# One more chunk's low weight parts by VectorE, and two ScalarE copies emitted later, in a gated mix of attention and GEGLU

## The chip, the cores and the metric

The kernel runs on one core of one Trainium2 chip. The metric is the device time of one execution in microseconds (us); less is better. Three runs of the kernel before took 595.72, 596.25 and 597.62 us, so the median is 596.25 us. The profile shows one further execution. In its lines PE is TensorE (PEld its weight loads), DVE is VectorE, ACT is ScalarE, POOL is GpSimd, and SP is the engine that only issues transfers. L689 is line 689 of the kernel before.

## The reference

For 2048 tokens of 512 channels the kernel computes a sliding, dilated attention (32 heads of 16 channels, 8 keys per token at a distance of 2), a GEGLU feed-forward network of 1792 hidden channels, and a gate that mixes them:

```python
g = _sigmoid((x * gate_w).sum(-1, keepdims=True))
a = _A_ref(x, A_wqkv, A_wo)          # attention and its output projection
b = (_gelu(x @ w_gate) * (x @ w_up)) @ w_down
return g * a + (1 - g) * b
```

All tensors are float32.

## The kernel before

**Tokens and parities.** The 2048 tokens are split into two halves by the parity of their position, since the keys of a token have its parity. Each half goes through the same stages: keys and queries, values (with the gate's logits), then the feed-forward network. `par` is 0 in the first parity and 1 in the second. The main function calls `values(0, ...)`, `ffn(0)`, `keys(...)` (for the second parity), `values(1, ...)` and `ffn(1)` in this order.

**Products.** Each block product is done with seven products of half the size instead of eight, from sums of quarters of both operands (names such as t1, t2, b11 for the weights, a11, s1 for the tokens). Each operand is kept as two numbers: a rounded high part, and a low part, raw minus high. A product takes three matmuls: high by high, high by low, low by high.

**Low parts, two ways.** `operands(par, f, i)` (L662 to L693) makes the weights of chunk f of the feed-forward network (14 chunks, f from 0) from the raw quarters in a tile `raw`. Group i = 0 has three quarters (768 columns), group i = 1 has four (1024 columns). In one way, ScalarE makes the high part (L678) and VectorE subtracts it from raw (L682). In the other, which this text calls "by transfer", ScalarE writes minus the high part into the place of the low part (L686), a GpSimd-issued transfer of 512 KB adds raw to it in memory (L689), and ScalarE makes the high part (L691). The function is a generator: the second half, after `yield`, is emitted at a later step. In the second parity, group 0 is loaded back from memory instead, where the first parity left it. Low parts of the hidden values (L749, L750 or L753) and of the down weights (L716, L718 or L720, L721) are made in the same two ways.

**Feed-forward.** `gate_up` (L794 to L845) works through one chunk: seven products on TensorE (`product`, L730), with evictions from PSUM by ScalarE (L735, L741, L812, L827, L843) and sums and products by VectorE (L742, L746). Between the products come pieces of other work: in chunks 0 and 1 the last two key products (`key_one`, matmuls at L460, evicted at L480 into a buffer `rt` and added into memory by two GpSimd-issued transfers, L465 and L466), and later `down` (L766, matmuls at L777), which multiplies hidden values by the down weights. The last group of `down` in the first parity scales its result by 1 - g while evicting it (L785) into a buffer that is then stored.

**Keys of the second parity.** `keys` (L416) follows the first parity's `down`. Its first product uses the four PSUM banks called `acc` (24 matmuls at L460), which are copied to four banks called `p` (L434, ScalarE); the second product (24 matmuls, `p<-d,A`) adds to these copies, and is evicted at L437. There are four `acc` and four `p` banks.

**Values.** `values` (L336 to L414) does seven products of four matmul groups each (matmuls at L348 with 258 columns; evictions by ScalarE at L355). After each of these 28 steps it calls `next(bg)`, so that a generator handed to it emits a little other work there. In the second parity this is `rest_b` (two steps), then empty steps, then `operands(1, 0, 1)`: the second group of chunk 0.

**Attention.** It runs on VectorE beside all this, as background work that is pulled in between (`pull`), with an exponential on ScalarE (L537).

**What sets the order.** The program is emitted in the order of the calls. A scheduler of the framework then decides, from costs of its own, in which order each engine gets its instructions; TensorE, VectorE and ScalarE run theirs strictly in that order, and so do the queues of the transfers. `paced` (L581) ties an instruction to the last matmul that was emitted before it, for the order only: the scheduler may not place it earlier than that. (In some stretches it also pins VectorE's instructions to their order of emission.) An instruction without it may be hoisted to any place where its operands and buffers allow.

Of the kernel before, what the change touches and what calls it, by code (L numbers as in the profile page):

```python
# [45 lines left out]
def tile_gated_mix(ctx: ExitStack, tc: tile.TileContext, xt, wqkv, wff, wo, out):  # L46
# [11 lines left out]
    def tl(tag, dt=F32):  # L58
        return pool.tile([P, COLS.get(tag, 512)], dt, name=tag, bufs=BUFS[tag])
# [151 lines left out]
    def room_b(name):  # L211
        if name in ("b11", "t2", "t4"):
            t = tl("g1", F32R)
            cols = [t[:, i * 512:(i + 1) * 512] for i in range(4)]
        else:
            cols = [*pair("d"), *pair("d")]
        for kc in range(2):
            QO[name, kc] = cols[2 * kc:2 * kc + 2]
# [7 lines left out]
    def split_b(name, kc):  # L226
        split(nc.vector, *QO[name, kc], QR[name, kc], held)
# [78 lines left out]
    def rest_b():  # L306
        room_b("b22")
        for kc in range(2):
            split_b("b22", kc)
            yield  # L310
# [270 lines left out]
    def paced(ins):  # L581

        if PIN[0] and ins.ins.engine == mybir.EngineType.DVE:
            tc.keep_in_program_order(ins)
        if not PACING[0]:
            return ins
        tc.add_manual_dep(ins.ins, LAST[-1].ins.name, mybir.DependencyInfo(mybir.DependencyClass.Sync,
                          mybir.DependencyReason.SCHED_ONLY), reason="pace")
        return ins
# [72 lines left out]
    def operands(par, f, i):  # L662


        n = len(GROUPS[i]) * QW
        w = tl(f"g{i}", F32R)
        hi, lo = w[:, :n], w[:, n:2 * n]
        for k, op in enumerate(GROUPS[i]):
            WG[f, op] = hi[:, k * QW:(k + 1) * QW], lo[:, k * QW:(k + 1) * QW]
        if par and not i:  # L670
            nc.sync.dma_start(w[:, :2 * n].bitcast(F32), WS[f, i])
            yield
            return
        raw = RAW[f][:, 3 * i * QW:][:, :n]
        if not i:
            KEEP[f] = w[:, :2 * n]
        if not i or (not par and f == 1):
            ins = nc.scalar.activation(hi, raw, AF.Copy)  # L678
            if f:
                paced(ins)  # L680
            yield
            ins = nc.vector.tensor_tensor(lo, raw, hi.bitcast(F32), op=OP.subtract)  # L682
            if f:
                paced(ins)
            return
        ins = nc.scalar.activation(lo, raw, AF.Copy, scale=-1.0)  # L686
        if par and not f:
            paced(ins)
        nc.gpsimd.dma_start(lo.bitcast(F32), raw, accum_op=OP.add)  # L689
        yield  # L690
        ins = nc.scalar.activation(hi, raw, AF.Copy)  # L691
        if par or f:
            paced(ins)  # L693
# [194 lines left out]
    def ffn(par):  # L888
        todo = iter(())
        for f in range(FC):  # L890
# [9 lines left out]
            if f + 1 < FC:  # L900
                for i in range(2):
                    steps = operands(par, f + 1, i)
                    at(1 + 2 * i, next, steps, None)
                    at(5 + i, next, steps, None)
                at(0 if f != 1 else 5, fetch_d, f + 1)
                for g_ in ((), (0, 1))[f] if f < 2 else (f,):
                    steps = down_w(par, g_)
                    at(2 if f > 2 else 4 - f % 2, next, steps, None)
                    at(7, next, steps, None)
            else:  # L910
                steps = down_w(par, f)
                at(1, next, steps, None)
                at(4, next, steps, None)
# [149 lines left out]
    for kc in range(KC):  # L1063
        name, i = ("b11", "b21")[kc // 2], kc % 2
# [134 lines left out]
    def first():  # L1199
        for _ in range(2):  # L1200
            yield
        combine(0)
        keep(0)
        for i in range(2):
            yield
            for _ in operands(0, 0, i):
                yield
        combine(1)
        fetch_d(0)
        yield  # L1210
        for n in "t1", "b22":
            room_b(n)
            for kc in range(2):
                if n == "t1":
                    combine_b("t1", "b11", "b22", "t2", kc)
                split_b(n, kc)
                yield
# [8 lines left out]
    def second():  # L1226

        yield from operands(1, 0, 0)
        room_v(*SMALL, *LARGE)
        for n in "b11", "b21", "t1", "b22", "t2":  # L1230
            fetch_v(n)
            yield
# [7 lines left out]
        if k < 2:  # L1240
            fetch_v(("t3", "t4")[k])

    values(1, chain(rest_b(), [None] * 9, operands(1, 0, 1)), again_v)
    ffn(1)


# [41 lines left out]
```

## Time and profile before

| what | value |
|---|---|
| three runs | 595.72, 596.25, 597.62 us |
| profiled execution | 596.87 us |
| its span, first to last instruction | 595.1 us |
| mean granted TensorE clock | 0.999 |
| VectorE busy | 533.3 us (90%) |
| L689 transfers (low parts by transfer) | 27, 512 KB each, median 6.1 us from issue to landing |
| L682 subtracts (low parts by VectorE) | 15, one of them 128x1024 |

The profiled execution's own time is 1.8 us longer than its span, and 0.62 us above the median of the three runs. A line of a timeline has the start, the duration, the engine, the line of the code, the operation, the output tile and its inputs, the shape, how many instructions run on without a break, and in brackets how long the engine was idle before it and what released it. On TensorE each matmul's duration overlaps the next one's; a new matmul of 512 columns starts every 0.227 us. On TensorE the first parity's feed-forward network runs from about 50 to 279 us, the second parity's keys (first five products) and values from 273 to 330 us, and its feed-forward network from 322 us on; they overlap somewhat at each change.

### The profile page before, as it was taken

To read this page: it belongs to the slowest core of one execution; us is meant where nothing else is said; L and a number is where in the kernel's file an instruction comes from. 1 tells how busy PE (TensorE), PEld (TensorE's weight loads), DVE (VectorE), ACT (ScalarE), POOL (GpSimd) and SP (SyncE) were. 2 spreads that over 40 slices of the span, in tenths; PEclk is the share of its full clock that TensorE was granted. 3 is DMA by queue.
4 is the path that set the end of the run, shared out by engine and by line. 5 is a ranking of instruction groups with operands and counts; after the bars stand their busy time and mean duration, and the time that the engine had idled before them with its cause. 6 is when DMAs were issued, how large, how long until landed. Compare 5 with 4: busy or idle time off the path is not lost.

```text
span 595.1 us, 8276 instructions
## 1 busy us (share of the span) xinstructions
PE 586.6 (99%) x2743; PEld 488.8 (82%) x2743; DVE 533.3 (90%) x622; ACT 429.4 (72%) x758; POOL 123.4 (21%) x144
## 2 busy tenths in 40 slices
PE   9999999999999999999999999999999999999997
PEld 7889887888888888887788888888888888888885
DVE  6989898999799996999996999799979988999891
ACT  6778786678887779777767665767696778796632
POOL 0130670112111112112001571112121212141200
PEclk9999999999999999999999999999999999999999
DMA  8689999989878988899889999889778988988725
GB/s 301 223 235 295 307 284 236 295 245 243 260 219 246 232 268 234 237 344 267 255 264 330 258 276 227 230 190 265 198 247 213 260 213 215 265 197 230 98 53 176
DMA packets 89464, 143.28 MB, mean 241 GB/s; under 512 B 8655, under 2 KB 49999, under 8 KB 89422
## 3 DMA queue, kind: packets, MB, share of 16 engines
q1 hardware_dynamic: 67470, 106.91, 54.6%
q0 software_dynamic: 21664, 35.46, 33.8%
q8 instruction: 21, 0.34, 0.3%
q10 hardware_dynamic: 288, 0.39, 0.2%
q14 instruction: 21, 0.17, 0.1%
HBM read 69.83 MB, written 46.49 MB: 195 GB/s over the span
## 4 chain that ended last, share of the span: by engine, by line
PE 90%; DMA 6%; DVE 1%; ACT 1%; issue 1%; SPq 0%; ACTq 0%; DVEq 0%
PE p L730 42%; PE p L777 13%; PE acc L777 12%; PE acc L460 10%; PE p L1002 5%; PE acc L348 3%; PE p L348 3%; DMA g<-raw 2%; PE acc L1002 2%; DMA v<-vs 1%; DMA raw<-ws 1%; PE p L460 1%; DMA vs<-hh 1%; DMA raw<-xt 1%; DVE raw L245 1%
## 5 line engine op out<-in xcount | busy, mean ns | idle before, releaser
L730 PE MATMUL p<-S,g 128*128 128x512 f32 x672 | 166.7, 389 | 0.0
L730 PEld LDWEIGHTS p<-S,g 128*128 128x128 f32 x672 | 126.0, 188 | 26.1
L730 PE MATMUL p<-A,g 128*128 128x512 f32 x504 | 125.1, 390 | 0.7 <-DMA g<-raw 0.7
L730 PEld LDWEIGHTS p<-A,g 128*128 128x128 f32 x504 | 94.3, 188 | 20.8 <-DMA g<-raw 1.1
L558 DVE TENSOR_TENSOR prod<-v,lg 128x2048 f32<-128x2048 f32 x32 | 72.9, 2279 | 0.8
L519 DVE TENSOR_TENSOR prod<-kq 128x2048 f32<-128x2048 f32 x32 | 72.9, 2278 | 0.6 <-DMA kq<-kq 0.3
L522 DVE TENSOR_REDUCE lg<-prod 128x128 f32<-128x2048 f32 x32 | 73.0, 2281 | 0.1
L777 PE MATMUL p<-d,hh 128*128 128x512 f32 x224 | 68.8, 389 | 0.0
L689 POOL DMA_DIRECT2D g<-raw x27 | 23.4, 867 | 188.9 <-ACT g L686 122.9
L741 ACT ACTIVATE c<-p 128x512 f32<-128x512 f32 x56 | 33.3, 597 | 38.9 <-PE p L730 38.6
L777 PE MATMUL acc<-d,hh 128*128 128x512 f32 x224 | 58.4, 390 | 0.0
L777 PEld LDWEIGHTS acc<-d,hh 128*128 128x128 f32 x224 | 42.0, 188 | 8.9 <-ACT hh L749 0.2
L777 PEld LDWEIGHTS p<-d,hh 128*128 128x128 f32 x224 | 42.1, 188 | 8.7
L742 DVE TENSOR_TENSOR c<-c,s 128x512 f32<-128x512 f32 x56 | 37.8, 683 | 5.6 <-ACT c L741 5.4
L777 PE MATMUL p<-d,hl 128*128 128x512 f32 x112 | 42.6, 389 | 0.0
L746 DVE TENSOR_TENSOR c<-c 128x512 f32<-128x512 f32 x56 | 38.3, 684 | 3.2 <-ACT c L843 3.1
L562 DVE TENSOR_TENSOR prod<-prod 128x1024 f32<-128x1024 f32 x32 | 39.1, 1221 | 0.3
L735 ACT ACTIVATE s<-p 128x512 f32<-128x512 f32 x56 | 33.0, 590 | 7.1 <-PE p L730 6.5
L721 POOL DMA_DIRECT2D d<-r x23 | 19.7, 858 | 86.6 <-ACT d L720 60.0
L460 PE MATMUL acc<-d,S 128*128 128x512 f32 x144 | 35.2, 390 | 0.6 <-ACT hh L1164 0.6
L790 ACT ACTIVATE rt<-p 128x512 f32<-128x512 f32 x48 | 28.1, 594 | 9.4 <-PE p L777 9.1
L777 PE MATMUL acc<-d,hl 128*128 128x512 f32 x112 | 34.5, 389 | 0.0
(220 smaller groups left out, 1065.0 us busy)
## 6 DMA issues: line engine op xcount, KB each, us to landing
g<-raw POOLq DMA_DIRECT2D x27, 512.0 KB, 6.1
ws<-g SPq DMA_DIRECT2D x14, 768.0 KB, 5.9
g<-ws SPq DMA_DIRECT2D x14, 768.0 KB, 7.0
r<-wff SPq DMA_DIRECT2D x28, 256.0 KB, 4.5
raw<-wff SPq DMA_DIRECT2D x14, 512.0 KB, 4.5
d<-r POOLq DMA_DIRECT2D x23, 256.0 KB, 6.5
ws<-raw SPq DMA_DIRECT2D x14, 384.0 KB, 4.9
raw<-ws SPq DMA_DIRECT2D x14, 384.0 KB, 4.9
```

The lines of the kernel that those rows point to most:

```text
L348: LAST[:] = [nc.tensor.matmul(ps[:, :n], x[:, ts], VO[b][w][:, kc * WQ:kc * WQ + n], start=first, stop=(kc == 1 and i == 2), skip_group_ch ...
L460: LAST[:] = [nc.tensor.matmul(ps, x[:, ts], w, start=(start and kc == i == 0), stop=(kc == 1 and i == 2), skip_group_check=True)]
L519: paced(nc.vector.tensor_tensor(prod, spans(k, jj), q[:, jj:jj + 2, None, :].to_broadcast([P, 2, W, UC]), op=OP.mult))
L522: nc.vector.tensor_reduce(two_of(lg, jj), prod.rearrange("p j w (h d) -> p (j w) h d", d=DH), axis=AX.X, op=OP.add)
L558: paced(nc.vector.tensor_tensor(prod.rearrange("p j w (h d) -> p (j w) h d", d=DH), spans(v, jj).rearrange("p j w (h d) -> p j w h d", d=D ...
L562: nc.vector.tensor_tensor(prod[:, :, :4], prod[:, :, :4], prod[:, :, 4:], op=OP.add)
L730: LAST[:] = [nc.tensor.matmul(ps, w_, a_, start=(start and kc == 0 and n == 0), stop=(kc == 1 and n == 2), skip_group_check=True)]
L741: nc.scalar.activation(c, ps, AF.Copy)
L742: nc.vector.tensor_tensor(c, c, s, op=OP.add)
L746: nc.vector.tensor_tensor(ge, ge, up, op=OP.mult)
L777: LAST[:] = [nc.tensor.matmul(pp, a[:, ts], w, start=(i == 0 and n == 0 and gr == 0), stop=(i == 1 and n == 2), skip_group_check=True)]
L1002: LAST[:] = [nc.tensor.matmul(pa, a, b, start=(first and n == 0), stop=(last and n == 2), skip_group_check=True)]
```

## The change

Three conditions are changed.

```diff
@@ operands(par, f, i)
-        if not i or (not par and f == 1):
+        if not i or (not par and 0 < f < 3):
             ins = nc.scalar.activation(hi, raw, AF.Copy)
             if f:
                 paced(ins)
@@
         ins = nc.scalar.activation(lo, raw, AF.Copy, scale=-1.0)
-        if par and not f:
+        if par and f < 2:
             paced(ins)
         nc.gpsimd.dma_start(lo.bitcast(F32), raw, accum_op=OP.add)
         yield
@@ main
-    values(1, chain(rest_b(), [None] * 9, operands(1, 0, 1)), again_v)
+    values(1, chain(rest_b(), [None] * 20, operands(1, 0, 1)), again_v)
```

The first makes the second group of chunk 2 in the first parity by VectorE, as chunk 1's is already: one L686, one L689 and one L691 less, one L678 and one L682 of 128x1024 more. The second ties chunk 1's negative copy in the second parity to the last matmul emitted before it, as chunk 0's is already. The third moves the first step of `operands(1, 0, 1)` (L686 and L689) from the 12th to the 23rd of the 28 steps of `values`, and its second step (L691) to the one behind. Since the scheduler orders the whole program anew, instructions that the diff does not name can change places too: the order differs from the first parity's early chunks on.

## The prediction

> **What bounds the kernel now.** First the page: busy time by engine, the granted clock over 40 slices, and the chain that ended last.
>
> ```profile
> PE 586.6 (99%) x2743; PEld 488.8 (82%) x2743; DVE 533.3 (90%) x622; ACT 429.4 (72%) x758; POOL 123.4 (21%) x144
> ...
> PEclk9999999999999999999999999999999999999999
> ...
> PE 90%; DMA 6%; DVE 1%; ACT 1%; issue 1%; SPq 0%; ACTq 0%; DVEq 0%
> ```
>
> TensorE (PE) is busy for 586.6 of 595.1 us at a full clock, and the change neither adds nor removes a matmul. So only 8.5 us of the span can move: gaps in front of matmuls, found by the waits of TensorE, four of them here.
>
> ```profile
> PE p L73 <- DVE warm L70: 1.0, 1, 1.0
> PE p L730 <- DMA g<-raw: 0.7, 1, 0.7
> PE p L460 <- ACT p L434: 0.6, 1, 0.6
> ...
> PE acc L348 <- ACT hh L355: 0.5, 1, 0.5
> ```
>
> Each is a single wait (the columns are total, number, longest); the first is the start of the kernel. On the second and the fourth the diff acts; at the third the order of instructions changes as a side effect. A gap costs more than its wait, because the pipe restarts, so I count from the slot in which the next matmul would have begun: one 128x512 matmul every 0.227 us (9 from 275.31 to 277.35, shown below), one 128x258 every 0.119 us (17 from 320.01 to 322.03).
>
> **Edit 1: chunk 2's low part by VectorE in the first parity.** It removes a ScalarE negative copy (L686), a POOL transfer (L689) and a ScalarE high copy (L691), and adds one high copy (L678) and one VectorE subtract (L682), all 128x1024. TensorE's timeline at the place:
>
> ```profile
> 90.74 0.61 PE L730 MATMUL p<-A,g 128*128 128x512 f32 x2
> 92.05 1.19 PE L730 MATMUL p<-A,g 128*128 128x512 f32 x4 [0.69 <-DMA g<-raw]
> 93.08 1.08 PE L777 MATMUL acc<-d,hh 128*128 128x512 f32 x4
> ```
>
> Two of six matmuls run, the third needs the low part. It should have started at 90.74 + 2 x 0.227 = 91.19 and started at 92.05: 0.86. The four then take 1.03 to the next row where 4 x 0.227 = 0.91 would do, a restart of about 0.1: 0.96 us in all. What it waited for, on ScalarE, POOL and VectorE:
>
> ```profile
> 78.37 1.08 ACT L686 ACTIVATE g<-raw 128x1024 fp32r<-128x1024 f32 x1
> ...
> 81.10 0.89 POOL L689 DMA_DIRECT2D g<-raw  x1 [1.99 <-DMA v<-vs]
> ...
> 81.67 0.68 DVE L657 TENSOR_TENSOR raw<-raw 128x512 f32<-128x512 f32 x1
> ...
> 90.94 0.69 DVE L538 TENSOR_REDUCE m<-lg 128x64 f32<-128x512 f32 x1 [2.04 <-ACT lg L537]
> ```
>
> The transfer was issued at 81.10 behind other POOL issues and its bytes were there only at about 92. With the change the high copy takes the slot at 78.37, and in the new VectorE order the subtract stands behind the L657 of 81.67. Its price comes from the one 128x1024 subtract of the run, the longest of this group:
>
> ```profile
> L682 DVE TENSOR_TENSOR g<-raw,g x15: 940/951/1217, 45.9 to 244.2; 128x768 fp32r<-128x768 f32 x14, 128x1024 fp32r<-128x1024 f32 x1
> ```
>
> So 1.22 us, done by 82.35 + 1.22 = 83.6. The new TensorE order wants chunk 2 somewhat earlier, its first low part about 89.4, which leaves 5.8 us: the 0.96 us goes. ScalarE saves one copy of 1.05 us, worth nothing, as it idles at most places. VectorE has 1.22 us more, covered by the 2.04 us idle at 90.94 (it waited there for ScalarE's exponential, not for its own work). Bounds: gain 0 to 0.96, cost 0 to 1.22 if the cover fails. I take -0.96.
>
> **Edits 2 and 3: the copies for chunks 0 and 1 in the second parity.** ScalarE runs in its fixed order; around 320 us it reads:
>
> ```profile
> 318.23 0.43 ACT L355 ACTIVATE hl<-p 128x256 f32<-128x256 f32 x1
> 321.16 1.06 ACT L686 ACTIVATE g<-raw 128x1024 fp32r<-128x1024 f32 x1 [2.49 <-DMA raw<-wff]
> 322.12 1.05 ACT L691 ACTIVATE g<-raw 128x1024 fp32r<-128x1024 f32 x1
> 323.07 0.36 ACT L355 ACTIVATE hh<-p 128x256 f32<-128x256 f32 x1
> ...
> 323.60 1.05 ACT L686 ACTIVATE g<-raw 128x1024 fp32r<-128x1024 f32 x1
> 324.55 0.38 ACT L355 ACTIVATE hl<-p 128x256 f32<-128x256 f32 x1
> ```
>
> Chunk 0's negative copy waits 2.49 us for its raw weights, and with L691 and chunk 1's L686 it holds up the evictions (L355) that free the banks of `values`. TensorE pays twice:
>
> ```profile
> 320.01 2.19 PE L348 MATMUL acc<-c,S 128*128 128x258 f32 x17
> 322.03 1.53 PE L730 MATMUL p<-A,g 128*128 128x512 f32 x6
> 323.76 0.99 PE L348 MATMUL acc<-c,S 128*128 128x258 f32 x6 [0.19 <-ACT hl L355]
> 325.25 2.42 PE L348 MATMUL acc<-c,A 128*128 128x258 f32 x18 [0.50 <-ACT hh L355]
> ...
> 333.69 1.52 PE L730 MATMUL p<-A,g 128*128 128x512 f32 x6
> ```
>
> Six matmuls of 0.227 from 322.03 end at 323.39: 0.37 lost. Six of 0.119 from 323.76 end at 324.47: 0.78. With one more restart behind, 1.25 us. In the new ScalarE order six more L355 stand ahead of chunk 0's L686, and chunk 1's comes after the first L480: the evictions follow the matmuls, and the 1.25 us goes. Bounds: 0 to 1.25.
>
> The price is lateness of chunk 0's transfer. The 17 matmuls end about 322.0, so I put L686 at 322.5 instead of 321.16 (estimate) and the POOL issue, 1.36 later as in the row below (322.52 - 321.16), at 323.86. The first use is the row at 333.69, which moves to 332.44 without the two gaps; the low part is its third matmul, 332.89. So the transfer has 9.03 us. POOL's issues, the DMA times of that window (318 to 350), and those of the line over the run:
>
> ```profile
> 322.52 0.88 POOL L689 DMA_DIRECT2D g<-raw  x1 [40.44 <-DMA c<-vwt]
> ...
> 332.06 1.21 POOL L465 DMA_DIRECT2D ks<-rt  x1 [6.25 <-ACT rt L480]
> ```
>
> ```profile
> g<-raw POOLq DMA_DIRECT2D x3, 512.0 KB, 7.5
> ```
>
> ```profile
> DMA to landing us min/median/max: 4.4/6.1/12.0
> ```
>
> At 7.5 it lands at 331.4, 1.5 us early: cost nothing. At the longest, 12.0, it lands at 335.9: +3.0 us. I take 0, because chunk 1's transfer, issued 2.4 us behind it before, now comes after the store of 332.06 and leaves it alone. [...]
>
> Chunk 1's transfer, issued about 333, lies among L465/L466 stores and has until about 348; at 12.0 it is there at 345. Cost nothing by itself; that it delays the stores and so the `rt` buffers is kept for a rival.
>
> **The side effect: the change of parity.** Comparing the instruction order of the two programs, I find one difference outside the diff's reach that counts. In the kernel before TensorE does this, and ScalarE beside it:
>
> ```profile
> 275.31 2.20 PE L460 MATMUL acc<-g,A 128*128 128x512 f32 x9
> 277.35 1.07 PE L777 MATMUL p<-d,hl 128*128 128x512 f32 x4
> 278.26 2.88 PE L460 MATMUL acc<-g,A 128*128 128x512 f32 x12
> 281.78 5.76 PE L460 MATMUL p<-d,A 128*128 128x512 f32 x24 [0.64 <-ACT p L434]
> 287.90 1.19 PE L460 MATMUL acc<-g,S 128*128 128x512 f32 x4 [0.36 <-ACT S L129]
> 289.29 3.92 PE L460 MATMUL acc<-g,S 128*128 128x512 f32 x16 [0.20 <-DVE S L88]
> ```
>
> ```profile
> 277.78 0.69 ACT L785 ACTIVATE s<-p,gc 128x512 f32<-128x512 f32 x1 [2.14 <-PE p L777]
> ...
> 281.11 2.07 ACT L434 ACTIVATE p<-acc 128x512 f32<-128x512 f32 x4
> ```
>
> The four last `down` matmuls (L777, hl) close four banks; ScalarE then scales them out (four L785, with two L129 between) and only then copies `acc` to the freed banks (L434), for which the 24 matmuls at 281.78 wait. From hl to L434 is a chain of 281.11 - 277.35 = 3.76 us, plus 0.67 to TensorE's start, and 12 matmuls (2.72 us) cover it all but 0.80. In the new order these 12 stand ahead of hl: hl moves to 277.35 + 2.72 = 280.07, directly followed by the 24. ScalarE's order there is unchanged, so L434 comes at 283.83, TensorE at 284.50, and the gap is 0.80 + 2.72 = 3.52 us. Part comes back: while TensorE stands, VectorE gets further with the low parts of S, so the second of the two gaps behind goes (four matmuls from 287.90 take 0.91, and the next starts at 289.29: 0.48); the first, behind a ScalarE copy that shifts along with L434, stays. Net +2.72 - 0.48 = +2.24. Bounds: 0 (something else covers it) to 2.72. I take 2.24, as nothing else stands between hl and the 24 in TensorE's order.
>
> **Sum.** -0.96 - 1.25 + 2.24 = +0.03 us. The profiled execution took 596.87 us (its span of 595.1 and 1.8 around it), 0.62 above the median of 596.25. So 596.9 on its scale, 596.3 on the median's.
>
> **Rivals.** What a measurement of this kernel tells from no change is about 0.3%, 1.8 us.
>
> A, faster: the parity change costs nothing and only the two gains stay: 596.25 - 2.21 = 594.0. For it: the gains are plain waits in the rows. Against: hl sits right before its consumer's chain. Chance 0.14.
>
> B, slower: chunk 0's low part is late in the second parity. It decides from a landing above 9.03 us; at 12.0 it adds 3.0: 596.3 + 3.0 = 599.3. For it: the longest row, and POOL's queue filled with stores from 332 on, to which chunk 1's transfer is now added. Against: 7.5 in this window. Chance 0.18.
>
> C, the change does not do what it says for chunk 2: VectorE reaches the subtract late, so the gap at 92 stays (+0.96), or its 1.22 us pushes the attention's softmax. 596.3 + 0.96 = 597.3, or 596.3 + 1.22 = 597.5. Against: VectorE is brought back to ScalarE's pace later anyway:
>
> ```profile
> 316.78 0.69 DVE L538 TENSOR_REDUCE m<-lg 128x64 f32<-128x512 f32 x1 [3.55 <-ACT lg L537]
> ```
>
> There 3.55 us of idle time absorb it. Chance 0.11.
>
> D, slower: the gap of 3.52 us costs clock. No wait of TensorE before is longer than 1.0 us, and its granted clock is 9 or more in every slice, so no row prices it. I bound it by nothing, as behind the gap at 92, and by the gap once more, 3.5 us, and take the middle, 1.7: 598.0. [...] Chance 0.05.
>
> **Numbers.** My forecast has 0.50, the rest (0.02) is open. Faster by over 0.3% (below 594.5) takes most of A and a little of the open rest: 0.14. Slower (above 598.0) takes B's upper part, some of C and D, and the case that the new order of the feed-forward chunks has waits I did not find: 0.33. Within: 0.53. The range runs from near A, 594.2, to B at its longest row, 599.3; the forecast's own is 595.3 to 597.6, from the lower end with half of the parity loss to the upper with C's price.
>
> **What would show it.** Right: no L730 wait for g<-raw near 92; no L348 wait for L355 near 323; a wait of the first L460 p<-d,A for L434 of about 3.4 us after four L777 hl; L689 for chunk 0 landed before its third matmul. Wrong: a short gap at the parity change (A), an L730 wait for g<-raw near 332 (B), an L682 as releaser near 89 (C), a granted clock below full after 284 (D), or waits in the feed-forward stretches, where there is none now.

## The result, and the profile after

Over 19 runs each the changed kernel took 599.56 us (597.38 to 601.0) and the kernel before 597.14 us (595.62 to 598.85): a ratio of 1.0033, 95% interval 1.0022 to 1.0044. By this ratio it is slower by about 2.0 us; the two medians lie 2.4 us apart. On the scale of the three runs that the prediction had (596.25 us) the ratio gives 598.2 us. That lies above the forecast of 596.3, within the range, and just inside the band above 598.0 to which the prediction gave 33 chances in 100.

The page of the changed kernel, as far as it answers to the lines shown of before, with its waits of TensorE below:

```profile
PE 586.8 (98%) x2743; PEld 489.8 (82%) x2743; DVE 535.2 (90%) x623; ACT 428.2 (72%) x757; POOL 122.6 (21%) x143
...
PEclk9999999999999999999899999999999999999999
...
PE 96%; ACT 1%; DMA 1%; SPq 0%; issue 0%; ACTq 0%
```

```profile
PE p L460 <- ACT p L434: 3.4, 1, 3.4
PE p L73 <- DVE warm L70: 1.0, 1, 1.0
PE acc L460 <- ACT hh L1164: 0.6, 1, 0.6
PE acc L460 <- ACT S L129: 0.4, 1, 0.4
PE acc L460 <- ACT g L87: 0.3, 1, 0.3
```

The wait for g<-raw and both waits of L348 for L355 are gone, and the wait for L434 has grown from 0.6 to 3.4 us. New is an 8 in the row of the clock. TensorE at the change of parity, then the granted clock in stretches of it (columns: stretch, its length, TensorE busy, clock, share and GB/s of the DMA engines):

```profile
272.21 3.79 PE L460 MATMUL acc<-g,A 128*128 128x512 f32 x16
275.83 1.98 PE L777 MATMUL p<-d,hh 128*128 128x512 f32 x8
277.65 1.98 PE L460 MATMUL acc<-g,A 128*128 128x512 f32 x8
279.46 1.07 PE L777 MATMUL p<-d,hl 128*128 128x512 f32 x4
283.89 7.17 PE L460 MATMUL p<-d,A 128*128 128x512 f32 x24 [3.36 <-ACT p L434]
291.43 4.87 PE L460 MATMUL acc<-g,S 128*128 128x512 f32 x20 [0.37 <-ACT S L129]
```

```profile
281.00:283.00 2.00, 0.00 (x0) 1.00 0.68 140
284.00:286.00 2.00, 2.00 (x5) 0.50 1.03 304
286.00:287.00 1.00, 1.00 (x3) 0.51 1.04 415
287.00:289.00 2.00, 2.00 (x10) 1.00 0.91 252
```

The four L777 stand right ahead of the 24 matmuls, as the order said. They need a low part `hl` that VectorE makes nearly 4 us later now; first the kernel before, then the changed one:

```profile
273.76 0.68 DVE L750 TENSOR_TENSOR hl<-c,hh 128x512 fp32r<-128x512 f32 x1
```

```profile
277.69 0.68 DVE L750 TENSOR_TENSOR hl<-c,hh 128x512 fp32r<-128x512 f32 x1
```

In the kernel before, the four subtracts for A and d came behind it; in the changed kernel they stand ahead of it. Behind the gap TensorE runs at half its clock until 287: five matmuls in 2 us where some nine would fit at 0.227 us each, and 7.17 us for 24 matmuls that took 5.76 before. The runs without a profile tell the same by their mean clock: the two of 19 with 1.000 took 597.38 and 597.65 us, the 17 with 0.997 or less 598.42 to 601.0.

To see where time comes and goes, I take the start of the n-th of the 2743 matmuls from each profile's timeline and subtract the same of the kernel before; the table has the change over each stretch, in us ("after" is the changed kernel). The first column is the time in the profile before at which the stretch ends.

| stretch, until | predicted | after | e1 | e2 | e3 | e4 | e5 | e12 |
|---|---|---|---|---|---|---|---|---|
| start to chunk 1, 72.4 | 0 | +0.33 | -0.02 | +0.63 | +0.64 | +0.23 | +1.81 | +0.32 |
| chunk 2, 118.7 | -0.96 | -0.97 | -0.98 | -0.12 | -0.97 | -0.82 | -0.98 | -0.98 |
| change of parity, 291.9 | +2.24 | +3.72 | +2.29 | +0.01 | +3.80 | +4.06 | +1.02 | +1.24 |
| keys and values, 322.3 | 0 | -0.29 | -0.16 | -0.23 | +0.07 | -0.29 | +0.17 | -0.21 |
| chunk 0's copies, 336.2 | -1.25 | -1.24 | 0.00 | -0.52 | -0.69 | -1.04 | -0.63 | -0.63 |
| the rest, 590.7 | 0 | 0.00 | -0.04 | +0.02 | +0.49 | +0.18 | +0.38 | +0.29 |
| sum | +0.03 | +1.55 | +1.09 | -0.21 | +3.34 | +2.32 | +1.77 | +0.03 |

The experiments e1 to e12 follow. The row of the parity change is the one that differs most from the forecast, by 1.48 us; the +0.33 of the start and the -0.29 of keys and values nearly cancel.

### The profile page after: what moved, and what is told of

Same layout as the page of the kernel before. It is cut to its first block, busy times and chain, and to the rows that moved or that the text cites. A ratio compares the mean times of both kernels' runs of the same rounds, so it can differ in the third digit from the quotient of the medians.

```text
span 596.6 us, 8268 instructions
## 1 busy us (share of the span) xinstructions
PE 586.8 (98%) x2743; PEld 489.8 (82%) x2743; DVE 535.2 (90%) x623; ACT 428.2 (72%) x757; POOL 122.6 (21%) x143
## 4 chain that ended last, share of the span: by engine, by line
PE 96%; ACT 1%; DMA 1%; SPq 0%; issue 0%; ACTq 0%
PE p L730 45%; PE acc L777 13%; PE p L777 13%; PE acc L460 10%; PE p L1002 5%; PE p L348 4%; PE acc L348 3%; PE p L460 2%; PE acc L1002 2%; DMA prod<-wqkv 1%; SPq L1072 0%; ACT A L129 0%; SPq L1069 0%; ACT d L87 0%; ACT c L785 0%
## 5 line engine op out<-in xcount | busy, mean ns | idle before, releaser
L777 PE MATMUL p<-d,hh 128*128 128x512 f32 x224 | 68.0, 389 | 0.0
L689 POOL DMA_DIRECT2D g<-raw x26 | 23.4, 900 | 188.7 <-ACT g L686 81.8
L777 PE MATMUL acc<-d,hh 128*128 128x512 f32 x224 | 58.8, 389 | 0.0
L777 PEld LDWEIGHTS acc<-d,hh 128*128 128x128 f32 x224 | 42.0, 188 | 8.9 <-ACT hh L749 0.2
L777 PEld LDWEIGHTS p<-d,hh 128*128 128x128 f32 x224 | 42.0, 188 | 8.7
L777 PE MATMUL p<-d,hl 128*128 128x512 f32 x112 | 42.0, 389 | 0.0
L460 PE MATMUL acc<-d,S 128*128 128x512 f32 x144 | 35.2, 390 | 0.6 <-ACT hh L1164 0.6
L777 PE MATMUL acc<-d,hl 128*128 128x512 f32 x112 | 35.0, 389 | 0.0
```

The lines of the kernel that those rows point to most:

```text
L460: LAST[:] = [nc.tensor.matmul(ps, x[:, ts], w, start=(start and kc == i == 0), stop=(kc == 1 and i == 2), skip_group_check=True)]
L777: LAST[:] = [nc.tensor.matmul(pp, a[:, ts], w, start=(i == 0 and n == 0 and gr == 0), stop=(i == 1 and n == 2), skip_group_check=True)]
```

## The experiments

My theory after the result: the two gains are real, the loss is the gap at the parity change, both come as forecast, and a lowered clock behind the gap adds what the sum lacked. The rivals: the loss comes from the second parity, or from the new order of the feed-forward part.

**e1: the first edit alone.**

```diff
-        if not i or (not par and f == 1):
+        if not i or (not par and 0 < f < 3):
```

> Only the first edit (chunk 2 by VectorE). In the instruction order it alone brings the 12 matmuls ahead of the last four L777. Theory (the loss is the gap at the parity change plus a lowered clock behind it, both from edit 1): wait for g<-raw near 92 gone (-0.96), wait of L460 p<-d,A for L434 about 3.4 us (+2.24), granted clock below full behind it (+1.5): +2.8 us, ratio 1.0047. Rival (the loss comes from edits 2 and 3, the parity gap is paid back): -0.96 us, ratio 0.9984.

Measured: 600.09 us against 596.97, ratio 1.0051 (1.0034 to 1.0068). The gap is there with edit 1 alone; the profiled execution happens to be one whose clock stayed full, so it shows the gap by itself:

```profile
279.12 1.07 PE L777 MATMUL p<-d,hl 128*128 128x512 f32 x4
283.54 5.74 PE L460 MATMUL p<-d,A 128*128 128x512 f32 x24 [3.36 <-ACT p L434]
289.64 5.77 PE L460 MATMUL acc<-g,S 128*128 128x512 f32 x24 [0.36 <-ACT S L129]
```

The same gap of 3.36 us, but 24 matmuls in 5.74 us behind it. In the table the parity change costs 2.29 us here and 3.72 in the changed kernel: the difference, 1.43 us, is the clock. The six runs say it too: two with a mean granted clock of 0.999 or more took 597.97 and 598.55 us, the four of 0.997 and less 600.05 to 601.47. The rival (-0.96 us) falls. A run with the lowered clock took about 2 us longer here than one without, more than the 1.43 between the two profiles.

**e2: edits 2 and 3 without the first.**

```diff
-        if par and not f:
+        if par and f < 2:
...
-    values(1, chain(rest_b(), [None] * 9, operands(1, 0, 1)), again_v)
+    values(1, chain(rest_b(), [None] * 20, operands(1, 0, 1)), again_v)
```

> Only edits 2 and 3 (ScalarE's copies in the second parity later). Theory: the two L348 waits for L355 near 323 go, the parity change is as before, clock full: -1.25 us, ratio 0.998. Rival (these edits make a transfer late or crowd POOL's queue): +1 to +3 us, ratio 1.002 to 1.005, with a wait of L730 for g<-raw near 332 or 350.

Measured: 596.52 us against 596.97, ratio 0.9992 (0.9978 to 1.0005). No loss, and no wait for a late low part in the second parity. The gain is 0.5 us of the 1.25 that were expected, too small for these runs to tell from none. The profile shows a new wait:

```profile
323.27 1.33 PE L730 MATMUL p<-A,g 128*128 128x512 f32 x5
324.93 3.23 PE L348 MATMUL acc<-c,A 128*128 128x258 f32 x24 [0.33 <-DMA c<-vwt]
```

The waits for L355 are gone, but a transfer with weights of `values` (c<-vwt) is late by 0.33 us. It is no slower than in the changed kernel: it lands 5.7 us after its issue at 319.08, and there 5.9 us after 319.80. But TensorE is ready for it 5.35 us after the issue here, and 7.1 us there.

**e3: all edits, and the low part of the last hidden values early.** Order-only dependencies hold the second half of the first key product behind the last four L777, and copies and subtracts of the weights behind those of the last hidden values.

```diff
+    END = []
+    def behind(ins, first):     # order only
+        tc.add_manual_dep(ins.ins, first.ins.name, mybir.DependencyInfo(mybir.DependencyClass.Sync,
+                          mybir.DependencyReason.SCHED_ONLY), reason="behind")
@@ split; in the same way held, with END[0]
+        if END:
+            behind(ins, END[1])
@@ hidden
+            if not par and key == (FC - 1, 1):
+                END.extend(ends_)
@@ keys, the first product's second half: each of its matmuls
+        down_last = LAST[-1]
+                if after:
+                    behind(LAST[0], after)
```

> All three edits, and order-only dependencies that put the last four L777 (hl) ahead of 12 of the L460 matmuls again, with the hl parts made early enough. Theory: gap before L460 p<-d,A back to about 0.8 us, clock full, gains of 0.96 and 1.25 stay: -2.2 us, ratio 0.9963. Rival (the clock falls or time goes elsewhere in the changed order also without the gap): ratio 0.999 to 1.002.

Measured: 599.83 us against 596.97, ratio 1.0047 (1.0031 to 1.0063). The wait for L434 went, and others took its place:

```profile
281.49 5.75 PE L474 MATMUL p<-d,A 128*128 128x512 f32 x24 [0.25 <-ACT p L448]
289.13 1.20 PE L474 MATMUL acc<-g,S 128*128 128x512 f32 x4 [1.89 <-ACT S L137]
291.18 5.06 PE L474 MATMUL acc<-g,S 128*128 128x512 f32 x14 [0.86 <-DVE S L94]
```

(Lines are shifted in this kernel; L474 is L460 of before.) In the new order ScalarE made two later weights (d) ahead of the first S, where before has one. Nine of ten runs have a clock of 0.997 or less, although no wait is longer than 1.89 us. That the gap was only moved tells nothing for or against the rival about the feed-forward part; it needed e5 and e12.

**e4: the gap shortened by three matmuls.** All edits, with three of the 24 matmuls held behind the four L777.

```diff
+                key_mm(ps, t, a, b, (1,) if k == 0 else (0, 1), False,
+                       down_last if k == 0 and t > 2 else None)
```

> All three edits, and 3 of the 24 L460 matmuls held behind the last four L777, so the gap is shorter by 3 x 0.227: about 2.7 us of wait instead of 3.4. [...] Rival (a gap of nearly 3 us lowers the clock as well): clock about 0.997, +0.8 us, ratio 1.0014.

Measured: 599.85 us against 596.97, ratio 1.0045 (1.0031 to 1.0058); clock 0.997 in all five runs. The gap is 2.68 us, and the clock falls all the same:

```profile
281.00:283.00 2.00, 0.00 (x0) 1.00 0.59 140
284.00:286.00 2.00, 2.00 (x8) 0.59 1.04 396
286.00:287.00 1.00, 1.00 (x4) 0.50 0.87 352
287.00:289.00 2.00, 2.00 (x8) 0.80 0.72 220
```

Here TensorE starts again at 283.27. The mean of 0.59 from 284 to 286 says that the half clock began only at about 284.4, 1.1 us after the work. The rival is right about the clock: a wait of 2.68 us went with a lowered one in each of the five runs. The gap is shorter, but TensorE then waits 1.21 us for S at 291.81, so the parity change costs more than in the changed kernel (+4.06 us in the table).

**e5: all edits in the order of before.** As e3, and the copies and subtracts of d also held behind those of S, and two evictions of the second key product (L437) behind copies of S.

```diff
+            END[:] = S2                 # the last copy and subtract of s2
             split_b("t3", kc)
+            END.clear()
@@ keys, evictions of k == 1: t = 1 and 2 behind the first and second copy of s2
+                    if k == 1 and t in EVB:
+                        behind(ins, SA[EVB[t]])
```

> All three edits, and order-only dependencies that bring back the order of before at the parity change on all three engines: the last four L777 ahead of 12 L460 matmuls, the copies and subtracts of S ahead of the later ones of d. Theory (all of the loss is the gaps at the parity change and the clock behind them): gaps between 281 and 292 at most the 1.85 us of before, clock 0.999 or more, the gains of 0.96 and 1.25 stay: -2.2 us, ratio 0.9963. Rival (the changed order of the feed-forward part loses by itself): gaps and clock as said, but ratio 0.999 or more.

Measured: 597.89 us against 596.86, ratio 1.0004 (0.9986 to 1.0021). The long gap is gone, the clock is full in nine of twelve runs, but a wait of 1.60 us for S remains, and it comes from VectorE:

```profile
277.37 2.28 DVE L548 TENSOR_REDUCE lg<-prod 128x128 f32<-128x2048 f32 x1
279.57 0.68 DVE L94 TENSOR_TENSOR A<-raw,A 128x512 fp32r<-128x512 f32 x1
...
288.59 0.68 DVE L257 TENSOR_TENSOR raw<-raw 128x512 f32<-128x512 f32 x1
```

```profile
289.31 0.63 ACT L138 ACTIVATE S<-raw 128x512 fp32r<-128x512 f32 x1 [1.77 <-DVE raw L257]
```

VectorE has no idle moment from 277 to 290, and an attention step of 2.28 us stands ahead of the sums that S needs. So neither expectation was met as written: the ratio is that of the rival, but the waits are not those of before. They come to 1.84 us here (0.24 and 1.60) and to 1.20 there (0.64, 0.36 and 0.20), so the theory was not put to its test. The table splits it: -0.98 in chunk 2, +1.02 at the parity change, -0.63 at chunk 0, +0.38 in the rest. The kernel e6, in the order of before, shows +0.30 in that last row too, so that row doesn't tell for the rival about the feed-forward part. +1.81 of this execution is the start of the kernel, where the 41st matmul comes 1.95 us later than in the profile before.

**e6, e7, e8: the kernel before with a longer gap.** The first of the four last L785 is repeated once, twice and four times; nothing is left out, as it writes the same again.

```diff
-            nc.scalar.activation(st, pp, AF.Copy, scale=gc[:, par, jj:jj + 1])
+            for _ in range(2 if jj == BT else 1):      # 3 in e7, 5 in e8
+                nc.scalar.activation(st, pp, AF.Copy, scale=gc[:, par, jj:jj + 1])
```

(In e7 and e8 an order-only dependency also keeps L434 behind the repeats.)

> The kernel before, with the first of the four last L785 done twice, so that L434 comes 0.57 us later: gap of about 1.4 us instead of 0.8, nothing else changed. [...]

> The kernel before with that L785 done three times: gap of about 1.9 us. [...]

> The kernel before with that L785 done five times: gap of about 3.1 us. [...]

Measured: e6 1.0022 (1.0000 to 1.0044), e7 1.0011 (0.9991 to 1.0031), e8 1.0053 (1.0035 to 1.0071), all against 596.86 us. What the profiles and the runs show of gap and clock, with the other kernels, in order of the longest wait behind the L777:

| kernel | wait there, us | runs with clock 0.997 or less |
|---|---|---|
| before, beside e1 to e12 | 0.64 | 6 of 80 |
| e6 | 1.22 | 2 of 10 |
| e5 | 1.60 | 3 of 12 |
| e7 | 2.06 | 4 of 10 |
| e3 | 1.89 and 0.86 | 9 of 10 |
| e4 | 2.68 | 5 of 5 |
| e1, after | 3.36 | 4 of 6, 17 of 19 |
| e8 | 3.50 | 6 of 6 |

The kernel before needs nothing of the change to lose the clock, only the gap: e8 took 3.50 us of wait in its profile and fell to half clock behind it, and all six runs have a lowered mean clock.

```profile
285.69 7.17 PE L466 MATMUL p<-d,A 128*128 128x512 f32 x24 [3.50 <-ACT p L438]
```

The number of lowered runs grows from a few at one microsecond to nearly all from 2.7 on; the 2 of 10 of e6 can't be told from the 3 of 31 that the kernel before had beside it. (e8 also had a wait of 1.5 us for g<-raw in chunk 2, so not all of its 1.0053 is the gap.)

**e9: less attention work at the change of parity.** As e5, with

```diff
-            pull(n * PACE[par] * (1.0 if par or f + 1 < FC else 0.8))
+            pull(n * PACE[par] * (1.0 if par or f + 1 < FC else 0.4))
...
-                pull((0.2, 0.2, 0.6, 1.2, 1.2)[k])
+                pull((0.0, 0.0, 0.6, 1.2, 1.2)[k])
```

> All three edits, the order-only dependencies of the kernel called all edits, order of before, and less attention work pulled in during the last chunk of the first parity and the first two key products (factors 0.8 to 0.4, and 0.2 to 0), so that VectorE makes the sums and low parts of S before the next attention step. Theory (the wait for S left in that kernel is VectorE's attention steps of 2.28 us in front of the sums): no wait above 0.6 us between 281 and 292, clock full, the gains of 0.96 and 1.25 stay, and about 1 us of the 1.85 of before goes too: -3.2 us, ratio 0.9946. Rival (the attention pushed back is missed later): the gaps go, and TensorE waits for as much elsewhere, ratio 0.998 to 1.001.

Measured: 604.62 us against 597.29, ratio 1.0115 (1.0087 to 1.0144). At the parity change it does what the theory says, and TensorE is 2.28 us ahead of the kernel before at the 1620th matmul. The rival is right about the rest:

```profile
281.16 5.73 PE L484 MATMUL p<-d,A 128*128 128x512 f32 x24 [0.64 <-ACT p L456]
...
594.10 1.22 PE L1030 MATMUL p<-S,hh 128*128 128x512 f32 x2 [5.02 <-ACT hh L93]
```

The attention that was pushed back is missed at the very end: VectorE finishes its last step (the transpose, L571 of before) at 587.23 instead of 580.95 in the changed kernel, its result comes back from memory 5.02 us too late for TensorE, and two of the last matmuls take 1.22 us where two took 0.62. The loss is far above the rival's 0.998 to 1.001. This way of moving VectorE's work found no free place for it.

**e10 and e11: the second and the third edit alone**, one execution each.

> Only the second edit (chunk 1's copy tied to the last matmul). One look, to be read from the profile: chunk 0's copies still stand ahead of evictions, so the first L348 wait near 323 stays, and the second (325.25) shrinks by up to the 1.05 us of the copy moved away: total of the two waits 0.2 to 0.4 us instead of 0.69. If chunk 0's copies alone make both waits: 0.6 to 0.7.

> Only the third edit (the empty steps). One look, to be read from the profile: the evictions stand ahead of both copies, so no L348 wait for L355 near 323. If chunk 1's untied copy still holds up the last evictions: one wait of 0.3 to 0.6 us stays.

Of the kernel with edit 2 alone:

```profile
PE acc L348 <- ACT hl L355: 0.3, 1, 0.3
```

The kernel with edit 3 alone has no wait of L348 in its list. So the 20 empty steps remove both waits, and the tie of chunk 1's copy removes one of the two when alone. The stretch of chunk 0's copies is shorter by 0.67 us with edit 2 alone and by 0.79 with edit 3 alone. Both still wait for chunk 2's transfer, 1.0 and 0.9 us.

**e12: VectorE gets its 1.22 us back.** All three edits, and

```diff
-LOWS = (4, 8, 10), (4, 6, 8, 10, 12)
+LOWS = (4, 8, 10, 12), (4, 6, 8, 10, 12)
```

> All three edits, and VectorE gets its 1.22 us back elsewhere: chunk 12's two low hidden parts in the first parity (two L750 subtracts of about 0.6 us of VectorE each) are made by transfer (L753) instead. In the instruction order this alone brings back the order of before at the parity change on TensorE, ScalarE and VectorE: 12 L460 matmuls behind the last four L777. Theory (the order moved because VectorE had 1.22 us more; gap and lowered clock are all of the loss): gap of about 0.8 us there, clock 0.999 or more in most runs, the gains of 0.96 and 1.25 stay: -2.2 us, ratio 0.9963. Rival (the reordered feed-forward part or the two transfers cost as much as is gained): the gap goes, but ratio 0.999 to 1.001, with waits of L777 for hl or d transfers.

Measured: 598.47 us against 597.49, ratio 1.0013 (0.9997 to 1.0029); the clock is 0.999 or more in eleven of twelve runs. The order at the parity change is that of before, with nothing forced, and the gap with it. One of the two new transfers is late:

```profile
265.30 1.20 PE L777 MATMUL acc<-d,hl 128*128 128x512 f32 x4 [0.64 <-DMA hl<-c]
...
277.91 1.07 PE L777 MATMUL p<-d,hl 128*128 128x512 f32 x4
278.82 2.88 PE L460 MATMUL acc<-g,A 128*128 128x512 f32 x12
282.34 1.89 PE L460 MATMUL p<-d,A 128*128 128x512 f32 x7 [0.64 <-ACT p L434]
```

In the table that costs +1.24 us, more than chunk 2 gains. VectorE makes the last `hl` at 273.70 here, as before. So 1.2 us less work for VectorE is enough to bring the order back, although it was given back in another chunk than it was taken from; that the order follows VectorE's work by the scheduler's costs is argued from this and e1, not shown. The rival is right about the sum, and no kernel here is faster than both. The profiled execution (596.90 us) is the second fastest of its twelve; what the others lose beyond it was not seen.

## Why the prediction was right, and where it was not

**Chunk 2 (edit 1), -0.96 forecast.** Right: -0.97 in the changed kernel (the wait alone was 0.69 us), -0.97 or -0.98 in e1, e3, e5 and e12, and -0.82 in e4. VectorE made the subtract where the order said:

```profile
82.53 0.68 DVE L657 TENSOR_TENSOR raw<-raw 128x512 f32<-128x512 f32 x1
83.13 1.22 DVE L682 TENSOR_TENSOR g<-raw,g 128x1024 fp32r<-128x1024 f32 x1
...
93.34 0.69 DVE L538 TENSOR_REDUCE m<-lg 128x64 f32<-128x512 f32 x1 [0.39 <-ACT lg L537]
```

It is done at 84.3, and of the idle time at L538 0.39 us are left of 2.04, as the cover that was named. Rival C did not come. But "covered" was said of the place only: the 1.22 us came back as another order nearly 200 us later, which e1 and e12 bear out. The prediction had found that order and its price, not its cause.

**Chunks 0 and 1 (edits 2 and 3), -1.25 forecast.** Right in the changed kernel: -1.24. The estimate of where chunk 0's copy comes was 322.5; with 2.79 us by which TensorE is late there, 325.3:

```profile
325.30 1.06 ACT L686 ACTIVATE g<-raw 128x1024 fp32r<-128x1024 f32 x1
```

```profile
326.66 0.88 POOL L689 DMA_DIRECT2D g<-raw  x1 [42.47 <-ACT hl L355]
```

The transfer landed 5.4 us after its issue, so the 9.03 us were enough, and TensorE did not wait for the low part: rival B did not come. In e2, e3, e5 and e12 only 0.5 to 0.7 us of the gain are seen; in each of them the transfer c<-vwt is late next, by 0.2 to 0.33 us of wait. From the matmul ahead of this wait to the one behind it TensorE takes 0.56 to 0.73 us there, and 0.23 in the changed kernel; two slow steps right behind add 0.17. That is 0.50 to 0.67 us of the 0.55 to 0.72 that are missing, so this transfer explains nearly all of it.

**The change of parity, +2.24 forecast.** The chain was right, from the last L777 through four L785 to L434: the gap of 3.36 us and the second wait for S gone; +2.29 in e1, where the clock stayed full. Rival A did not come.

**What failed: rival D, and with it the sum.** The prediction gave the clock 5 chances in 100, and took no term for it. It came in 17 of 19 runs. Its price of 1.7 us was about right (1.43 between the profiles of after and e1, about 2 between the runs of either kernel with and without it); the half clock lasts 3.41 us in after, from 283.57 to 286.98. The chance was the author's estimate, and no run shows it: the gap of 3.36 us lowered the clock in 21 of the 25 runs of after and e1, a wait of 2.68 us in five runs of five, one of 2.06 in four of ten. The failed step is therefore the chance, and with it the missing term. No row of before had priced such a gap; with the bounds of nothing and 3.5 us that the prediction had itself set, the middle, 1.7, belonged in the sum as an unknown cost, and the forecast would have been 598.0.

So the forecast of no change was off by one term: +0.03 and 1.48 us is +1.51, and the profiled spans differ by 1.5 (595.1 and 596.6). The runs differ by more, 2.0 us by the ratio: the profiled execution (598.42 us) is the fastest of the 17 with a lowered clock. It has one stretch of half clock (0.997). Two of the 19 runs are at 0.993 and took 600.47 and 600.82 us; where they lost more was not seen, as only one execution has a profile. That the measured time lies inside the range is luck: the range was drawn that wide for other slow cases, not for this one.

What stays open: why c<-vwt has less of a lead in e2, e3, e5 and e12, and whether a version with both gains and the gap of before exists. The one way tried that needs no VectorE (e12) lost it in a transfer.

## What to carry to other kernels

Where one engine is the bound and another is nine tenths busy, 1 us more on the second can cost nothing in its place and, as here, several at a later place where both meet: compare the order of instructions there, not only at the edit. A gap in front of TensorE like those measured here (the clock was lowered in 4 of 10 runs with a wait of 2.06 us, in 21 of 25 with 3.36) is to be priced with its length and, by its chance of a half clock, 1.4 to 2 us more. To close it, look for the chain that it waits for and for what the engines of that chain do before; in every try here, moving the work of a full engine only moved the wait.

## What the runs showed of the hardware

**The clock.** In four profiles it falls at the parity change, to 0.50 and for 3.4 us: in after from 283.57 to 286.98, in e3, e4 and e8, by the means of stretches of 1 us, from about 291.8, 284.4 and 285.4 on. It can fall as late as 1.1 us after TensorE works again (e4). The waits of TensorE there, and where the clock fell:

| profile | wait of TensorE, us | half clock from |
|---|---|---|
| e8 | 3.50, to 285.69 | 285.4 |
| after | 3.36, to 283.89 | 283.57 |
| e1 | 3.36, to 283.54 | full |
| e4 | 2.68, to 283.27 | 284.4 |
| e7 | 2.06, to 283.32 | full |
| e3 | 1.89, to 289.13, and 0.86, to 291.18 | 291.8 |

So the length of a wait does not decide alone: the same 3.36 us left the clock full in the profile of e1 and not in that of after, and 2.06 us left it full in e7 where 1.89 and 0.86 did not in e3. What decides it was not shown, nor why the runs of one kernel differ, as each kernel has one profile. What the runs give is the share of lowered ones, from 2 of 10 at 1.22 us (e6) to 21 of 25 at 3.36 and 6 of 6 at 3.50.

**What the mean clock says.** Part of it is the tail, in which TensorE has no work left: in the profile before its last matmul starts at 590.70 us, and the clock falls to 0.50 at 594.14. So the 0.999 of this profile is no loss, and the runs of the changed kernel at 0.995 and 0.996 (599.12 to 599.93 us) took no longer than many at 0.997 (598.42 to 601.0).

**The start.** It alone varies by 1.9 us: the 41st matmul comes at 7.10 us in the profile before and at 9.05 in that of e5. In e5 the first seven 128x512 matmuls take 3.35 us, from 5.04 us on; in the profile before the first 13 take 3.89 us, from 4.30 on. A gain of 1 us can't be read from the time of one execution, but it can from the stretch that it belongs to.
